# Block A's seven-product stage: one order in all groups, narrow columns first for three row pairs, weight and row sums in small parts

## The chip, the core and the metric

The kernel runs as one program on one core of a Trainium2 chip. The metric is the device time of one execution in microseconds. A core has five engines that run their own instruction queues side by side: TensorE (PE in the profile) multiplies matrices into eight PSUM banks, VectorE (DVE), ScalarE (ACT) and GpSimd (POOL) work elementwise, and SyncE (SP) issues the transfers between HBM and the on-chip memory. Each queue is worked off in order; an instruction that waits for another engine holds up all that stands behind it in its own queue.

## What is computed

Two attention blocks with 2048 rows, width 640 and 32 heads of 20, whose outputs stand side by side. Block A looks at eight earlier rows at distance 2, block B at all rows.

```
qkv = (x @ wqkv).reshape(B, S, 3, H, Dh)          # both blocks
A: logits[s, w] = q[s] . k[s - 2 w] * Dh**-0.5,  w = 0..7;  softmax over w;  o = sum attn * v
B: scores = q k^T * Dh**-0.5;  softmax over all keys;  o = p @ v
out = concat([o_A @ wo_A, o_B @ wo_B], axis=-1)
```

## The kernel before

Every matrix product is done in three passes, because a float32 value is kept as a rounded part ("hi") and a remainder ("lo"): hi*hi, hi*lo and lo*hi (`PASSES`). ACT casts the hi part and DVE subtracts it to get the lo part (`lo_of`); a pair of such instructions stands wherever an operand is prepared.

The program has, in this order: block A's projection `x @ wqkv` for the first 12 of 16 row tiles (the loop over `a_steps`), block B's query and key projection, its value projection, and then a long loop over block B's scores, maxima, exponentials and products, beside which POOL computes block A's window attention.

The change touches the first of these alone. There the columns of `wqkv` are held as two weight sets: `WP[0]` (W0, two halves of 512 columns) and `WP[1]` (W1, the narrow one, two halves of 448). The rows are held as six row pairs `XA[0..5]`, 256 rows each, two tiles of 128. The first 8 steps project the first two row pairs with W0 in the plain way. All that follows is done by `a_quad`, once for a row pair and a weight set: ten groups, each a 2x2 block product with seven products in place of eight. It needs sums of weight chunks (`ACols.sums`, four DVE instructions for each of two chunk pairs), their hi and lo parts (`ACols.second`: two casts on ACT, two remainders on DVE), the same of the rows (`ARows.sums`, `ARows.second`) and the parts of the unsummed rows (`ARows.base`: three casts, three remainders).

A group has 54 matmuls. By the names of the products, with the matmuls in each: A11 B11 (6), which ACT copies to `c[0]`; S4 with B22 (9); S2 T2 (6), after which DVE sets `c[1] = c[0] + b[1]`; A12 with B21 (9), into the bank that ACT has copied, and a store; S1 T1 (6), `c[1] += b[2]` and a store; S3 T3 (6), added in PSUM to the bank of S2 T2, `c[0] += b[1]`; then the last rows' chunk (three matmuls, added to the bank of S1 T1) and a store, and A22 with T4 (9) and a store. So S3 waits for DVE's first addition and the last chunk's three matmuls for its second. In the first group (`late`) A12 stands before S2.

A step (`n`) is what lies between two `yield`s of a group: four to a group, steps 8 to 11 are group 0, 12 to 15 group 1, and so on; step 47 is the last. One more place, "between", lies behind a group's first product, with `n` still that of the step before. Which preparation stands at which step is written out by hand, in the loop over `a_steps`: it sets where in the queues of ACT, DVE and SP the pieces come, in front of or behind the group's own copies and additions. A tile that is stored (`ro`) goes to DRAM one step later through SP's queue; three buffers hold them. The buffers "vb", two in number, are shared by the loaded rows (`stg`) and the weights' sums (`x_sums`). Two chunks of late weight columns are loaded in the stage (`late_w`, tile `wt`), cast some steps later, and stored with the rest of the weights (`keep`) for later use.

In the profile all recorded instructions carry line 61, that of the helper which records them, so they are told apart by tile: `sum` is c[0] or c[1], `wc` and `wl` weight parts, `wr` and `sums` weight sums, `xn` row parts, `stg` loaded rows.

Of the kernel before, what the change touches and what calls it, by code (L numbers as in the profile page):

```python
# [9 lines left out]
F32 = mybir.dt.float32  # L10
F32R = mybir.dt.float32r
AF = mybir.ActivationFunctionType
ALU = mybir.AluOpType
# [8 lines left out]
KC = 5  # L22
# [43 lines left out]
def attention_pair(ctx, tc, xa, wqk_a, wv_a, wo_a, xb, wqk_b, wv_b, wo_b, oa, ob):  # L66
# [3 lines left out]
    sb = ctx.enter_context(tc.tile_pool(name="sb", bufs=1))  # L70
# [3 lines left out]
    dve, act = InOrder(tc, nc.vector, 0.075, 960), InOrder(tc, nc.scalar, 0.111, 1400)  # L74
# [151 lines left out]
    class ARows:  # L226


        def __init__(self, p, raw=None):
            self.p, self.raw, self.rest = p, raw, None  # L230

        def load(self):
            self.raw = sb.tile([128, KC, 256], F32, tag="vb", bufs=2, name="stg")
            sp.dma_start(self.raw, xa[:, self.p * 256:self.p * 256 + 256].rearrange("(k p) c -> p k c", p=128))

        def parts(self, u, k, src):
# [24 lines left out]
            self.parts(self.u, 4, self.raw[:, 1:KC - 1:2, 128:])  # L261
            self.parts(self.u, 6, self.raw[:, KC - 1].rearrange("p (t c) -> p t c", t=2))

        def sums(self):
            ev, od = (self.raw[:, o:KC - 1:2] for o in range(2))
            a11, a12, a21, a22 = ev[:, :, :128], od[:, :, :128], ev[:, :, 128:], od[:, :, 128:]
            dve.tensor_tensor(a22, a21, a22, ALU.add)
            dve.tensor_tensor(a21, a11, a21, ALU.subtract)
            dve.tensor_tensor(a11, a22, a11, ALU.subtract)
            dve.tensor_tensor(a12, a12, a11, ALU.subtract)  # L270

        def second(self):
            hi, lo = (self.u[:, i, 8:].rearrange("p (k t) c -> p k t c", t=2) for i in range(2))
# [13 lines left out]
    class ACols:  # L287
# [65 lines left out]
            self.one(self.b11[kp], self.raw[2 * kp][:, 0])  # L353
            self.one(self.odd[kp], self.raw[2 * kp + 1])

        def sums(self, kp, x):

            ev, od = self.raw[2 * kp:2 * kp + 2]
            x = x[:, :, :self.n]
            dve.tensor_tensor(x[:, 0], ev[:, 1], ev[:, 0], ALU.subtract)  # L360
            dve.tensor_tensor(x[:, 1], od[:, 1], ev[:, 1], ALU.subtract)
            dve.tensor_tensor(od[:, 1], od[:, 1], x[:, 0], ALU.subtract)
            dve.tensor_tensor(od[:, 0], od[:, 0], od[:, 1], ALU.subtract)

        def second(self, kp, x):

# [40 lines left out]
    def product(p, xs, ws, start, stop):  # L407

        for n, (x, w) in enumerate(zip(xs, ws)):
            for i, (wi, xi) in enumerate(PASSES):  # L410
                pe.matmul(p, x(xi), w(wi), start=start and n == i == 0, stop=stop and n == len(ws) - 1 and i == 2,
                          skip_group_check=not start)

    def a_store(g, t, op, *srcs):

        r = sb.tile([128, WA], F32, tag="ao", bufs=3, name="ro")
        c, end = AC[g], AC[g + 1]
        op(r[:, :end - c], *(u[:, :end - c] for u in srcs))
        hf, r0 = divmod(t * 128, HS)
        while c < end:  # L420
            m, c1 = divmod(c, D)
            n = min(D - c1, end - c)
            dst, pad = ((qa_d, 0), (ka_d, PAD), (va_d, PAD))[m]
            after(1, sp.dma_start, dst[hf, pad + r0:pad + r0 + 128, c1:c1 + n], r[:, c - AC[g]:c - AC[g] + n])
            c += n

    def add(r, a, b):
        dve.tensor_tensor(r, a, b, ALU.add)
# [7 lines left out]
    def a_quad(X, W, late=False):  # L436

        n, t, g = W.n, 2 * X.p, 2 * W.P
        A11, A12 = ([X.rows(0, 2 * kp + o) for kp in range(2)] for o in range(2))
        A22 = [X.rows(1, 2 * kp + 1) for kp in range(2)]  # L440
        l1, l2 = ([X.rows(j, KC - 1)] for j in range(2))
        B11 = [W.cols(2 * kp, 0) for kp in range(2)]
        B21, B22 = ([W.cols(2 * kp + 1, j) for kp in range(2)] for j in range(2))
        b = [next_bank()[:, :n] for _ in range(5)]
        c = [sb.tile([128, 512], F32, tag=tag, bufs=2, name="sum")[:, :n] for tag in ("raw", "rb")]
        product(b[0], A11, B11, True, True)
        act.copy(c[0], b[0])
        yield True
        product(b[3], X.s(4) + l1, B22 + W.c[1], True, True)

        def c11():
            product(b[0], A12 + l1, B21 + W.c[0], False, True)
            a_store(g, t, act.copy, b[0])
        if late:
            c11()
            yield
        product(b[1], X.s(2), W.T(2), True, True)
        add(c[1], c[0], b[1])
        if not late:
            c11()  # L460
            yield
        product(b[2], X.s(1), W.T(1), True, True)
        add(c[1], c[1], b[2])
        a_store(g + 1, t, add, c[1], b[3])
        yield
        product(b[1], X.s(3), W.T(3), False, True)
        add(c[0], c[0], b[1])
        product(b[2], l2, W.c[1], False, True)
        a_store(g + 1, t + 1, add, c[0], b[2])
        yield  # L470
        product(b[4], A22 + l2, W.T(4) + W.c[0], True, True)
        a_store(g, t + 1, add, c[0], b[4])
        yield

    def store_rows(p, dst):
# [12 lines left out]
    XA = [ARows(p, r[0][:, 2:, p * 256:p * 256 + 256]) for p in range(2)]  # L488
    WP = [ACols(0, r[0][:, :2]), ACols(1, r[1][:, :2, :448])]
# [215 lines left out]
    def a_steps():  # L705

        W = WP[0]
        first = [next_bank() for _ in range(4)]
        for k in range(KC):
            W.half(k, 0)  # L710
            for x in XA:
                x.chunk(k)
            for c in PASSES:
                for t in range(4):
                    pe.matmul(first[t], XA[t // 2].rows(t % 2, k)(c[1]), W.cols(k, 0)(c[0]),
                              start=(k == 0 and c == PASSES[0]), stop=(k == KC - 1 and c == PASSES[-1]))
        for k in range(KC):
            W.half(k, 1)
        for x in XA:
            x.sums()  # L720
        for x in XA:
            x.second()
        for t in range(4):
            a_store(0, t, act.copy, first[t])
            yield
        for t in range(4):
            p = next_bank()
            product(p, [XA[t // 2].rows(t % 2, k) for k in range(KC)], [W.cols(k, 1) for k in range(KC)], True, True)
            a_store(1, t, act.copy, p)
            yield  # L730
        for p in range(2):
            yield from a_quad(XA[p], WP[1], not p)
        for p in range(2, UP // 2):
            for W in WP:
                yield from a_quad(XA[p], W)

    keeps = [(0, 0, 1), (0, 2, 1)]
# [3 lines left out]
    n = -1  # L741
    for between in a_steps():
        if between:
            if n == 7:
                WP[0].second(0, x_sums)
            elif n == 11:
                XA[2].base()
            continue
        tick()
        n += 1  # L750
        if n == 0:
            for j in range(2):
                WP[1].half(KC - 1, j)
        elif n == 1:
            WP[1].base(0)
            x_sums = sb.tile([128, 2, 512], F32, tag="vb", bufs=2, name="sums")
        elif n == 2:
            WP[1].sums(0, x_sums)
            WP[1].base(1)
        elif n == 3:  # L760
            WP[1].second(0, x_sums)
            WP[1].sums(1, x_sums)
        elif n == 6:
            WP[1].second(1, x_sums)
        elif n in (7, 8):
            WP[0].sums(n - 7, x_sums)
        elif n == 12:
            WP[0].second(1, x_sums)
        if n in (5, 13, 14, 21):
            XA.append(ARows(len(XA)))  # L770
            XA[-1].load()
        if n in (16, 24, 32):
            XA[n // 8 + 1].base()
        elif n in (12, 17, 25, 33):
            XA[n // 8 + 1].sums()
        elif n in (13, 18, 26, 34):
            XA[n // 8 + 1].second()
        if n in (33, 35):
            for c in range(n - 33, n - 31):
# [9 lines left out]
        if n in (16, 24):  # L789
            k = n // 4 - 4  # L790
            late_w = [sb.tile([128, WP[1].n], t, tag="aq", bufs=2, name="wt") for t in (F32, F32R)]
            sp.dma_start(late_w[0][:, :128], wv_a[0, :, k, 192:])
            sp.dma_start(late_w[0][:, 128:], wv_a[1, :, k])
        elif n in (20, 28):
            act.copy(late_w[1], late_w[0])
            lo_of(late_w[0].bitcast(F32R), late_w[0], late_w[1])
            late_w = [late_w[1], late_w[0].bitcast(F32R)]
        elif n in (21, 29):
            k = n // 4 - 5
            WP[1].b12 = {k // 2: late_w}  # L800
            WP[1].keep(k, 1)
        if n in (36, 37):
            pairs_x = [] if n == 36 else pairs_x
            pairs_x.append(x_raw(0, 2 * len(pairs_x), 2 * len(pairs_x) + 2, "vb", 2))
        elif n == 38:
            raw_m = [sb.tile([128, KC, 128], F32, tag="aq", bufs=2, name="stg") for _ in range(2)]
            for r, m in zip(raw_m, MS):
                sp.dma_start(r, wqk_b[m])
        elif n == 40:
            XB.append([big(0, [128, 2, KC - 1, 512], "xn"), None])  # L810
# [647 lines left out]
```

## Time and profile before

| | us |
|---|---|
| median of 3 runs | 1768.23 |
| lowest and highest | 1765.77, 1768.40 |
| the profiled execution | 1767.34 |
| its span, first to last instruction | 1765.6 |
| PE busy | 1739.2 |
| DVE, ACT, POOL busy | 1415.8, 1335.5, 1228.0 |

The seven-product groups run from about 33 to 168 us of the span; block B's projection begins at 168.21. The 40 slices of the page (44 us each) give the busy share in tenths; the stage lies in the first four.

```profile
PE   9899999999999999999999999999999999999999
PEld 7688888874445444444444444444444444444569
DVE  7545433689999999999999999999999999999400
ACT  6212322218998999999999999989999999989881
POOL 0000594495989888888898898988888898745442
PEclk9899999999999999999999999999999999999999
DMA  7468868784435563644474446536552635222223
```

A busy PE is not yet a PE at its full rate: a matmul's length is modelled, and the row PEclk says what clock was granted. A wait is given with the engine and the tile that ended it.

### The profile page before, as it was taken

Reading aid. Unit: us, or ns where it says so; the run is one execution under the profiler, and the core shown is the slowest. Engines: PE = TensorE matmul, PEld = TensorE weight load, DVE = VectorE, ACT = ScalarE, POOL = GpSimd, SP = SyncE. Lnnn points to the kernel's source line nnn. Section 1 sums busy time; section 2 is a strip of 40 time slices with the busy share of each in tenths; the row PEclk is TensorE's granted clock in tenths of the full one; section 3 lists DMA queues with packets and bytes.
Section 4 is the critical chain, followed back from the end, with each engine's and each line's share of the span. In section 5 each row is a group of like instructions: output and inputs, shape, how many; then the busy total and the mean of one; then the engine's idle time right before and its main releaser. Section 6 shows DMA issues by size and latency. Waiting matters only on the chain.

```text
span 1765.6 us, 32050 instructions
## 1 busy us (share of the span) xinstructions
PE 1739.2 (99%) x11271; PEld 991.9 (56%) x11271; DVE 1415.8 (80%) x1944; ACT 1335.5 (76%) x2601; POOL 1228.0 (70%) x1086
## 2 busy tenths in 40 slices
PE   9899999999999999999999999999999999999999
PEld 7688888874445444444444444444444444444569
DVE  7545433689999999999999999999999999999400
ACT  6212322218998999999999999989999999989881
POOL 0000594495989888888898898988888898745442
PEclk9899999999999999999999999999999999999999
DMA  7468868784435563644474446536552635222223
GB/s 228 144 201 268 311 245 269 228 258 114 150 115 158 136 183 114 156 144 133 137 187 139 133 148 155 166 100 173 140 165 90 147 106 144 60 73 62 61 71 111
DMA packets 220920, 270.19 MB, mean 153 GB/s; under 512 B 92748, under 2 KB 141400, under 8 KB 220760
## 3 DMA queue, kind: packets, MB, share of 16 engines
q1 hardware_dynamic: 220184, 267.50, 51.4%
q8 instruction: 88, 1.44, 0.3%
q14 instruction: 72, 0.59, 0.1%
q10 hardware_dynamic: 576, 0.66, 0.1%
HBM read 193.33 MB, written 74.74 MB: 152 GB/s over the span
## 4 chain that ended last, share of the span: by engine, by line
PE 91%; DVE 4%; DMA 1%; ACT 1%; issue 1%; SPq 1%; POOL 0%; DVEq 0%; ACTq 0%; POOLq 0%
PE ps_st L61 91%; DVE mx L61 2%; DMA bk<-kb_d 1%; SPq L61 1%; ACT e L61 1%; DVE wl L61 1%; DVE wr L61 0%; DMA wr<-wqk_a 0%; ACT wc L61 0%; DVE sums L61 0%; DVE xn L61 0%; DVE wc L61 0%; DMA rb<-s_d 0%; DVE sum L61 0%; POOL braw L61 0%
## 5 line engine op out<-in xcount | busy, mean ns | idle before, releaser
L61 DVE TENSOR_REDUCE mx<-ps_st 128x1 f32<-128x512 f32 (+1 forms) x1500 | 1217.5, 877 | 75.9 <-PE ps_st L61 65.6
L61 ACT ACTIVATE e<-ps_st 128x512 f32<-128x512 f32 x2048 | 1067.3, 609 | 34.0 <-PE ps_st L61 15.2
L61 PE MATMUL ps_st<-bq,bk 62*128 62x512 f32 x2048 | 610.7, 439 | 0.2
L61 PE MATMUL ps_st<-bk,bq 60*128 60x512 f32 x2048 | 556.9, 435 | 3.1 <-DMA bq<-qb_d 1.3
L61 PEld LDWEIGHTS ps_st<-bq,bk 62*128 62x128 f32 x2048 | 288.2, 184 | 478.4 <-ACT e L61 336.9
L61 PE MATMUL ps_st<-e,vb 128*32 128x512 f32 x4096 | 542.9, 604 | 2.1
L61 POOL TENSOR_TENSOR braw<-braw,more 128x512 f32<-128x512 f32 x224 | 287.7, 1284 | 145.6 <-ACT more L61 129.9
L61 POOL TENSOR_TENSOR akv<-akv 128x640 f32<-128x640 f32 (+3 forms) x304 | 282.1, 928 | 23.8
L61 PEld LDWEIGHTS ps_st<-bk,bq 60*128 60x128 f32 x2048 | 265.5, 184 | 35.8 <-DVE mx L61 12.0
L61 POOL TENSOR_TENSOR akv<-akv,aq 128x1280 f32<-128x1280 f32 x64 | 188.1, 2939 | 22.8 <-DMA akv<-ka_d 22.7
L61 PEld LDWEIGHTS ps_st<-e,vb 128*32 128x32 f32 x4096 | 82.0, 108 | 156.1 <-issue 71.0
L61 POOL TENSOR_TENSOR akv<-akv,al 128x1280 f32<-128x1280 f32 x64 | 152.1, 2376 | 0.2
L61 PE MATMUL ps_st<-wc,xn 128*128 128x512 f32 (+1 forms) x544 | 138.8, 388 | 13.4 <-DVE sum L61 12.1
L61 ACT COPY ro<-ps_st 128x320 f32<-128x320 f32 (+2 forms) x102 | 45.8, 451 | 137.0 <-PE ps_st L61 120.0
L61 ACT COPY more<-ps_st 128x512 f32<-128x512 f32 x224 | 132.5, 591 | 1.7 <-PE ps_st L61 1.4
L61 PE MATMUL ps_st<-ww,xn 128*128 128x320 f32 x768 | 125.8, 314 | 0.5 <-ACT e L61 0.5
L61 PEld LDWEIGHTS ps_st<-ww,xn 128*128 128x128 f32 x768 | 113.5, 188 | 20.8 <-ACT e L61 8.8
L61 PEld LDWEIGHTS ps_st<-wc,xn 128*128 128x128 f32 x544 | 104.8, 194 | 31.8 <-DVE sum L61 15.1
L61 POOL MEMSET ve<- 128x347 f32 x4 | 1.4, 391 | 168.4 <-DVE ro L61 156.7
L61 PE MATMUL ps_st<-xn,w 128*128 128x512 f32 x480 | 115.4, 389 | 0.0
L61 PEld LDWEIGHTS ps_st<-xn,w 128*128 128x128 f32 x480 | 90.0, 188 | 18.8 <-issue 0.2
L61 ACT CAST pr<-ps_st 128x512 fp32r<-128x512 f32 x40 | 23.5, 587 | 97.3 <-PE ps_st L61 93.1
(91 smaller groups left out, 1119.7 us busy)
## 6 DMA issues: line engine op xcount, KB each, us to landing
akv<-ka_d SPq DMA_DIRECT2D x128, 320.0 KB
akv<-va_d SPq DMA_DIRECT2D x128, 320.0 KB
wx<-wa_d SPq DMA_DIRECT2D x24, 480.0 KB
kb_d<-pr SPq DMA_DIRECT2D x20, 512.0 KB
qb_d<-pr SPq DMA_DIRECT2D x20, 512.0 KB
bk<-kb_d SPq DMA_DIRECT2D x16, 640.0 KB
bq<-qb_d SPq DMA_DIRECT2D x64, 160.0 KB
rb<-s_d SPq DMA_DIRECT2D x128, 64.0 KB
```

The lines of the kernel that those rows point to most:

```text
L61: return self.tc.keep_in_program_order(op(*a, **k))
```

## The change

Three things change, all in the seven-product stage. In every group the last two pieces change places: A22 with T4 stands before the last chunk's three matmuls. The third row pair, like the first two, takes W1 before W0, so that W0's sums are needed one group later. And the preparation moves to other steps: W1's last part behind group 0's first product; W0's four parts, which stood in groups 0 and 1, to steps 9 to 17, with one of the sums split in two; the rows' `base`, `sums` and `second` to behind the first product and the two steps after it, in the group before they are used; a row pair's buffer is taken apart from its load; the late columns' casts come one step earlier; some loads of block B's rows move by one to three steps.

```diff
-            for W in WP:
+            for W in (WP if p > 2 else WP[::-1]):
                 yield from a_quad(XA[p], W)
...
         add(c[0], c[0], b[1])
+        product(b[4], A22 + l2, W.T(4) + W.c[0], True, True)
+        a_store(g, t + 1, add, c[0], b[4])
+        yield
         product(b[2], l2, W.c[1], False, True)
         a_store(g + 1, t + 1, add, c[0], b[2])
-        yield
-        product(b[4], A22 + l2, W.T(4) + W.c[0], True, True)
-        a_store(g, t + 1, add, c[0], b[4])
         yield
...
         if between:
             if n == 7:
-                WP[0].second(0, x_sums)
+                WP[1].second(1, x_sums)
             elif n == 11:
                 XA[2].base()
+                XA[2].sums()
+            elif n == 15:
+                WP[0].sums(1, x_sums, 0)
+            elif n in (19, 27, 35):
+                XA[(n + 1) // 8 + 1].base()
             continue
...
         elif n == 1:
             WP[1].base(0)
+            XA.append(ARows(2))
+            XA[2].buffer()
             x_sums = sb.tile([128, 2, 512], F32, tag="vb", bufs=2, name="sums")
...
-        elif n == 6:
-            WP[1].second(1, x_sums)
-        elif n in (7, 8):
-            WP[0].sums(n - 7, x_sums)
+        elif n == 9:
+            WP[0].sums(0, x_sums)
         elif n == 12:
-            WP[0].second(1, x_sums)
-        if n in (5, 13, 14, 21):
+            XA[2].second()
+        elif n == 16:
+            WP[0].sums(1, x_sums, 1)
+        elif n in (14, 17):
+            WP[0].second(n // 17, x_sums)
+        if n in (13, 18, 23):
             XA.append(ARows(len(XA)))
+            XA[-1].buffer()
+        if n in (5, 13, 18, 23):
             XA[-1].load()
-        if n in (16, 24, 32):
-            XA[n // 8 + 1].base()
-        elif n in (12, 17, 25, 33):
+        if n in (20, 28, 36):
             XA[n // 8 + 1].sums()
-        elif n in (13, 18, 26, 34):
+        elif n in (21, 29, 37):
             XA[n // 8 + 1].second()
...
-        elif n in (20, 28):
+        elif n in (19, 27):
             act.copy(late_w[1], late_w[0])
...
-        if n in (36, 37):
-            pairs_x = [] if n == 36 else pairs_x
+        if n in (34, 38):
+            pairs_x = [] if n == 34 else pairs_x
...
-        elif n == 38:
+        elif n == 39:
             raw_m = [sb.tile([128, KC, 128], F32, tag="aq", bufs=2, name="stg") for _ in range(2)]
```

In `ACols.sums` and `ARows.sums` a parameter `part` picks the first two or the last two of the four instructions.

How the queues move is seen best in three places. On ACT, around the first product of group 0 (`sum` is its copy, the casts of 896 are W1's second part, those of 1024 W0's):

```order
 L61 CAST wc<-wr 128x896
 L61 CAST wc<-sums 128x896
-L61 COPY ro<-ps_st 128x512 x3
+L61 COPY ro<-ps_st 128x512 x4
+L61 COPY sum<-ps_st 128x448
 L61 CAST wc<-wr 128x896
 L61 CAST wc<-sums 128x896
-L61 COPY ro<-ps_st 128x512
-L61 COPY sum<-ps_st 128x448
-L61 CAST wc<-wr 128x1024
-L61 CAST wc<-sums 128x1024
```

The copy of the first product now stands ahead of the second pair of W1's casts, and W0's casts have left this place.

On DVE, in group 0 (`wl` of 896 are W1's remainders, `sums` and `wr` of 512 the sums of W0, `sum` and `ro` of 448 the group's own additions):

```order
 L61 TENSOR_TENSOR wl<-sums,wc 128x896
+L61 TENSOR_TENSOR sum<-sum,ps_st 128x448 x2
+L61 TENSOR_TENSOR ro<-sum,ps_st 128x448
 L61 TENSOR_TENSOR sums<-wr 128x512 x2
 L61 TENSOR_TENSOR wr<-wr,sums 128x512
 L61 TENSOR_TENSOR wr<-wr 128x512
-L61 TENSOR_TENSOR wl<-wr,wc 128x1024
-L61 TENSOR_TENSOR wl<-sums,wc 128x1024
-L61 TENSOR_TENSOR sums<-wr 128x512 x2
-L61 TENSOR_TENSOR wr<-wr,sums 128x512
-L61 TENSOR_TENSOR wr<-wr 128x512
-L61 TENSOR_TENSOR sum<-sum,ps_st 128x448 x2
```

The group's first two additions, which stood behind two parts of sums and one of remainders of W0, now stand ahead of all of them.

On PE, at the end of a W1 group (`wl` is the third pass of a T product; before, the first three of the five are the last chunk's):

```order
 L61 MATMUL ps_st<-wl,xn 128x448
-L61 MATMUL ps_st<-wc,xn 128x448 x5
-L61 MATMUL ps_st<-wl,xn 128x448
-L61 MATMUL ps_st<-wc,xn 128x448 x2
-L61 MATMUL ps_st<-wl,xn 128x448
-L61 MATMUL ps_st<-wc,xn 128x448 x3
+L61 MATMUL ps_st<-wc,xn 128x448 x2
+L61 MATMUL ps_st<-wl,xn 128x448
+L61 MATMUL ps_st<-wc,xn 128x448 x2
+L61 MATMUL ps_st<-wl,xn 128x448
+L61 MATMUL ps_st<-wc,xn 128x448 x6
```

The last chunk's three matmuls have gone from the front of the piece to its end, behind the nine of A22 with T4. Behind the stage, the rows of all engines are the same as before.

More of the change, by code (lines that the diff above doesn't have):

```diff
@@ L230, in __init__, with buffer @@
             self.p, self.raw, self.rest = p, raw, None
+        def buffer(self):
+            self.raw = sb.tile([128, KC, 256], F32, tag="vb", bufs=2, name="stg")
         def load(self):
-            self.raw = sb.tile([128, KC, 256], F32, tag="vb", bufs=2, name="stg")
             sp.dma_start(self.raw, xa[:, self.p * 256:self.p * 256 + 256].rearrange("(k p) c -> p k c", p=128))
@@ L262, in base, with sums @@
             self.parts(self.u, 6, self.raw[:, KC - 1].rearrange("p (t c) -> p t c", t=2))
-        def sums(self):
+        def sums(self, part=None):
             ev, od = (self.raw[:, o:KC - 1:2] for o in range(2))
             a11, a12, a21, a22 = ev[:, :, :128], od[:, :, :128], ev[:, :, 128:], od[:, :, 128:]
[L267 to L270, printed above, removed]
+            if part != 1:
+                dve.tensor_tensor(a22, a21, a22, ALU.add)
+                dve.tensor_tensor(a21, a11, a21, ALU.subtract)
+            if part != 0:
+                dve.tensor_tensor(a11, a22, a11, ALU.subtract)
+                dve.tensor_tensor(a12, a12, a11, ALU.subtract)
         def second(self):
@@ L354, in base, with sums @@
             self.one(self.odd[kp], self.raw[2 * kp + 1])
-        def sums(self, kp, x):
+        def sums(self, kp, x, part=None):
             ev, od = self.raw[2 * kp:2 * kp + 2]
             x = x[:, :, :self.n]
[L360 to L363, printed above, removed]
+            if part != 1:
+                dve.tensor_tensor(x[:, 0], ev[:, 1], ev[:, 0], ALU.subtract)
+                dve.tensor_tensor(x[:, 1], od[:, 1], ev[:, 1], ALU.subtract)
+            if part != 0:
+                dve.tensor_tensor(od[:, 1], od[:, 1], x[:, 0], ALU.subtract)
+                dve.tensor_tensor(od[:, 0], od[:, 0], od[:, 1], ALU.subtract)
         def second(self, kp, x):
```

## The prediction

> **What bounds the kernel now.** I read the page first, for the engine that never rests, then who keeps that engine waiting.
>
> ```profile
> PE 1739.2 (99%) x11271; PEld 991.9 (56%) x11271; DVE 1415.8 (80%) x1944; ACT 1335.5 (76%) x2601; POOL 1228.0 (70%) x1086
> ...
> PE ps_st L61 <- DVE sum L61: 12.1, 6, 5.8
> ```
>
> The first row is of the page, the second of the view of waits (in all, times, longest). PE is the bound. Among its waits, DVE's `sum` (the additions of the seven-product stage) has 12.1 us in six waits, the longest 5.8. The timeline of PE (start, length, instruction, idle time before) places them, and one more for a copy of ACT; of the four short ones the first and the last are shown:
>
> ```profile
> 32.20 4.56 PE L61 MATMUL ps_st<-wc,xn 128*128 128x512 f32 x21
> 38.06 2.50 PE L61 MATMUL ps_st<-wc,xn 128*128 128x448 f32 x11 [1.30 <-ACT sum L61]
> ...
> 48.38 1.12 PE L61 MATMUL ps_st<-wc,xn 128*128 128x448 f32 x2 [5.79 <-DVE sum L61]
> ...
> 52.21 0.37 PE L61 MATMUL ps_st<-wl,xn 128*128 128x448 f32 x1
> ...
> 53.02 4.21 PE L61 MATMUL ps_st<-wc,xn 128*128 128x448 f32 x20
> 57.08 0.36 PE L61 MATMUL ps_st<-wl,xn 128*128 128x448 f32 x1
> ...
> 66.31 2.23 PE L61 MATMUL ps_st<-wc,xn 128*128 128x448 f32 x5 [4.01 <-DVE sum L61]
> ...
> 75.42 0.39 PE L61 MATMUL ps_st<-wl,xn 128*128 128x512 f32 x1
> ...
> 81.76 1.43 PE L61 MATMUL ps_st<-wc,xn 128*128 128x512 f32 x5 [0.51 <-DVE sum L61]
> ...
> 117.32 1.28 PE L61 MATMUL ps_st<-wc,xn 128*128 128x448 f32 x5
> ...
> 123.72 0.39 PE L61 MATMUL ps_st<-wl,xn 128*128 128x512 f32 x1
> ...
> 154.37 1.45 PE L61 MATMUL ps_st<-wc,xn 128*128 128x512 f32 x5 [0.80 <-DVE sum L61]
> ```
>
> Idle: 1.30 + 12.1 = **13.4 us**, of which 5.79 and 4.01 are the long waits and 12.1 - 9.8 = 2.3 the four short ones. The two long waits cost more than their length, because matmuls behind them run slowly. The windows view (length, PE busy, PEld, DVE, ACT, POOL, granted clock, DMA share, GB/s) shows the clock:
>
> ```profile
> 48.40:52.20 3.80, 3.80 (x11) 3.46 (x12) 2.05 (x4) 0.00 (x0) 0.00 (x0) 0.57 0.16 60
> ...
> 66.30:72.00 5.70, 5.68 (x15) 4.97 (x16) 3.54 (x5) 0.51 (x1) 0.00 (x0) 0.50 0.67 198
> ...
> 38.00:168.20 130.20, 117.99 (x525) 101.44 (x526) 68.27 (x110) 27.24 (x46) 0.72 (x2) 0.95 0.60 193
> ...
> 168.20:304.00 135.80, 135.80 (x600) 112.50 (x600) 50.55 (x65) 37.72 (x61) 86.07 (x76) 1.00 0.80 279
> ```
>
> Full-clock spacing at 448 columns is (57.08 - 53.02) / 20 = 0.203 us. From 48.38 to 52.21 stand 11 matmuls, 3.83 us where 2.23 were due: 1.60 lost. From 66.31 to 75.42 stand 29 matmuls, 9.11 us; the same 29 of a later group take 123.72 - 117.32 = 6.40: 2.71 lost. Slow clock: **4.31 us**. The stage holds 13.4 + 4.31 = 17.7 us that a dense PE wouldn't need.
>
> [...]
>
> **The change, part by part.** The number of matmuls, additions and casts is the same; what changes is which of them stand in front of what.
>
> *The first copy (1.30).*
>
> ```profile
> 35.31 0.94 ACT L61 CAST wc<-wr 128x896 fp32r<-128x896 f32 x1 [3.01 <-DVE wr L61]
> 36.15 0.93 ACT L61 CAST wc<-sums 128x896 fp32r<-128x896 f32 x1
> ...
> 37.47 0.54 ACT L61 COPY sum<-ps_st 128x448 f32<-128x448 f32 x1
> ```
>
> ACT casts `W1.second(1)`, waits inside for DVE, and then copies the first product, for which PE waits. The change puts the copy ahead. PE's 21 matmuls end at 32.20 + 4.56 = 36.76 and the last nine (9 x 0.203 = 1.83) come behind the first product, which is thus ready at about 35.0; one `ro` copy and this one take about 1.1 us, done by 36.2. The wait goes. The casts follow until about 38.1, DVE's two remainders (1.09 each, as below) until about 39.3. The first is wanted 14 matmuls after 36.76, at 39.6, the second 1.2 us later; both are there over 1 us earlier.
>
> *The long wait (5.79 + 1.60).*
>
> ```profile
> 37.48 1.09 DVE L61 TENSOR_TENSOR wl<-sums,wc 128x896 fp32r<-128x896 f32 x1
> 38.60 1.29 DVE L61 TENSOR_TENSOR sums<-wr 128x512 f32<-128x512 f32 x2
> ...
> 47.10 0.69 DVE L61 TENSOR_TENSOR wr<-wr 128x512 f32<-128x512 f32 x1
> 47.71 1.34 DVE L61 TENSOR_TENSOR sum<-sum,ps_st 128x448 f32<-128x448 f32 x2
> ```
>
> From 38.60 to 47.71 DVE works on W0's weights, and only then adds what PE waits for. All of it moves behind. The S2 product then ends at 36.76 + 15 x 0.203 = 39.8, its addition (0.62) at 40.5, and S3, which adds into that bank, is due after six more matmuls, at 41.0. The wait goes, with 0.5 us to spare: the thinnest margin here.
>
> *The second long wait (4.01 + 2.71).*
>
> ```profile
> 56.13 1.36 DVE L61 TENSOR_TENSOR xn<-stg,xn 128x512 fp32r<-128x512 f32 x3 [1.62 <-ACT xn L61]
> ...
> 61.47 1.22 DVE L61 TENSOR_TENSOR wl<-wr,wc 128x1024 fp32r<-128x1024 f32 x1 [2.76 <-ACT wc L61]
> 62.79 1.23 DVE L61 TENSOR_TENSOR wl<-sums,wc 128x1024 fp32r<-128x1024 f32 x1
> 63.94 1.80 DVE L61 TENSOR_TENSOR stg<-stg 128x256 f32<-128x256 f32 x4
> ...
> 66.84 1.22 DVE L61 TENSOR_TENSOR xn<-stg,xn 128x1024 fp32r<-128x1024 f32 x1
> ```
>
> W0's remainders wait for ACT, then four row sums run, then the addition of group 1. After the change DVE has, from step 9 to step 17, two sums of W0 (2 x 2.6, 1.29 as at 38.60 and two of 0.69), two remainders (2 x 2.45), row pair 2 (1.36 + 1.80 + 1.22): 14.5 us. Its own work for a group is six of 0.62, 3.7 us. From step 9 of group 0 to step 17 of group 2 are about two groups of 54 x 0.203 = 11.0 us plus 2.5, less than 25 us, and they have to hold 14.5 + 2.2 x 3.7 = 22.7 us. It fits, at over 90%, so single additions will stand behind a piece of up to 2.45 us. Two things cover that: ACT, which makes the casts ahead of the remainders, is busy 27.24 us of 130.2, and in each group the nine matmuls of A22 (1.83) now stand between S3 and the last three, whose bank needs the addition. I take 0.4 us as left; the ends are 0 (all margins hold) and 6.7 (the same wait comes back whole).
>
> *The four short waits (2.3).*
>
> ```profile
> 79.74 1.36 DVE L61 TENSOR_TENSOR xn<-stg,xn 128x512 fp32r<-128x512 f32 x3 [2.46 <-ACT xn L61]
> 81.02 0.68 DVE L61 TENSOR_TENSOR sum<-sum,ps_st 128x512 f32<-128x512 f32 x1
> ```
>
> In each W0 group the three remainders of the next rows delay the two additions before the last product. The exchange puts nine matmuls, at least 9 x 0.203 = 1.8 us, in front of the matmuls that wait, at most 0.80 until now. They go. The next to be late would be S3, for the addition behind S2; from group 1 on it has fifteen matmuls of cover (nine of A12, six of S1), 3.0 us or more.
>
> *Transfers and later stages.* Behind the stage every engine has the same rows in the same order; POOL has no difference at all. PE is busy 135.80 of the next 135.80 us, so its end moves as the stage's end does, and nothing is given back unless data come late. DMA's work from 38.00 to 168.20 is 0.60 x 130.2 = 78 us; in 17.3 us less it is a share of 0.69. It is the burst that could bite:
>
> ```profile
> 169.51 0.62 ACT L61 CAST xl<-stg 128x512 fp32r<-128x512 f32 x1 [4.14 <-DMA stg<-xb]
> ...
> 171.00 0.84 PE L61 MATMUL ps_st<-xl,w 128*128 128x512 f32 x3
> ```
>
> The load for `xl` stands at the same step as before, so its lead stays; cast and remainder are done barely ahead of 171.00. Being later costs PE one for one; I take 0; the ends are 0 and 2, half of the 4.14 that ACT waits there.
>
> **Sum.** 13.4 + 4.31 - 0.4 = 17.3 us off the profiled execution's own 1767.34 (span 1765.6): 1750.0 us. The median of the runs is 1768.23, 0.9 above that execution, so the forecast against the median is 1750 to 1751; I say 1750.
>
> **The rivals.** *DVE or a load becomes the new wait (15 in 100).* Where the margins of 0.5 us break, part comes back. The other place is ACT's cast of the late weight columns, one step earlier than before:
>
> ```profile
> 79.64 0.88 SPq L61 DMA_DIRECT2D wt<-wv_a x2
> ...
> 91.36 0.57 ACT L61 CAST wt<-wt 128x448 fp32r<-128x448 f32 x1
> ...
> 147.49 0.49 SPq L61 DMA_DIRECT2D stg<-xb x1
> ...
> 153.48 1.05 ACT L61 CAST xn<-stg 128x1024 fp32r<-128x1024 f32 x1 [1.02 <-DMA stg<-xb]
> ```
>
> It came 11.7 us behind its issue; a step is (154.37 - 81.76) / 24 = 3.0 us, so 8.7 remain, and a 512 KB load took 5.5 (147.98 to 153.48). Behind the cast stands the copy of the next group's first product, with 15 matmuls (3.0) of cover. Both casts 3 us beyond that, or the wait of 4.01 with its 2.71 again, is 6 to 7 us: 1756.5. Against it speaks that each cover is longer than the rows it has to hide.
>
> *Slower (4 in 100): the order of stores.*
>
> ```profile
> 145.97 0.62 DVE L61 TENSOR_TENSOR ro<-sum,ps_st 128x448 f32<-128x448 f32 x1 [3.01 <-DMA va_d<-ro]
> ```
>
> DVE can stand at a store's buffer until an earlier store has left through SP's queue, and with it the additions behind. PE meets it at the next S3, 36 matmuls on, so it decides from 36 x 0.203 = 7.3 us; at 9.5 us in each of the eight later groups the gain is gone (8 x 2.2). If the shorter stage makes SP lag to 11.3 us, each loses 4.0 and, as behind the wait of 4.01, 2.7 of slow clock: 8 x 6.7 = 54 us, 1804. Against it: the longest such wait is 3.01, once, and it held up no matmul.
>
> *No change (4 in 100).* DVE's work is only moved, so the same 17 us of waiting could appear at the new places: about 1767. For it speaks DVE's over 90% in groups 0 to 2; against, the same DVE has 68.27 of 130.2 us in the whole stage.
>
> **Chances.** Forecast 77, partial 15, same 4, slower 4. A measurement of this kernel tells about 0.2% (3.5 us) from no change, so the partial case counts as faster: faster 92, same 4, slower 4. The range: down to 1747 (nothing left, and the fastest run lies 2.5 under the median), up to 1757 (the partial case); beyond it lie the last two cases and a tail.
>
> **What would show it.** Right: no wait of PE for `sum` above 1 us between 36 and 151; the granted clock 1.00 in that stretch; the first matmul of the next stage at about 151 instead of 168.21; later stages alike. Wrong: a wait for DVE between 40 and 65, a wait of ACT at `wt` that PE shares, or `xl` late at the stage's end.

## The result and the profile after

| | before | after |
|---|---|---|
| median, us | 1768.32 | 1749.12 |
| lowest and highest of 4 runs | 1765.77, 1768.56 | 1747.40, 1750.89 |
| the profiled execution | 1767.34 | 1747.40 |
| its span | 1765.6 | 1745.6 |

The time after is 0.9895 of the time before (0.9878 to 0.9912): 19.2 us less by the medians, where 17.3 were forecast against the profiled execution and 18.2 against the median. The forecast time, 1750, lies 0.9 above the median measured. Executions whose mean granted clock was 0.85 (one of the kernel before, 1868.31 us, and the profiled one of the exchange alone, 1861.01) are left out of every ratio, and the second is read for no length of the stage.

The page of the changed kernel shows the same work, and a whole clock in the first slices (the line of busy times, then the granted clock in the 40 slices):

```profile
PE 1733.5 (99%) x11271; PEld 988.5 (57%) x11271; DVE 1414.7 (81%) x1944; ACT 1335.8 (77%) x2601; POOL 1229.4 (70%) x1086
...
PEclk9999999999999999999999999999999999999999
```

PE's busy time fell by 5.7 us although the number of matmuls is the same: by the prediction's count 4.31 of that is the slow clock, which made matmuls long. The digit 8 in the second slice of PEclk is gone with it. The view of waits (in all, times, longest) has no row for DVE's `sum` any more; its longest is now one wait that was there before:

```profile
PE ps_st L61 <- POOL ident L61: 1.4, 1, 1.4
PE ps_st L61 <- DVE mx L61: 0.9, 2, 0.6
PE ps_st L61 <- DMA bq<-qb_d: 0.5, 1, 0.5
```

The timeline of PE (start, length, instruction) at the two ends of the stage: the last products of the plain steps with the first of group 0, and the first matmuls of block B's projection.

```profile
32.10 6.79 PE L61 MATMUL ps_st<-wc,xn 128*128 128x512 f32 x32
...
148.16 2.97 PE L61 MATMUL ps_st<-xn,w 128*128 128x512 f32 x12
150.96 1.11 PE L61 MATMUL ps_st<-xl,w 128*128 128x512 f32 x3
151.91 2.91 PE L61 MATMUL ps_st<-xn,w 128*128 128x512 f32 x12
154.66 0.84 PE L61 MATMUL ps_st<-xl,w 128*128 128x512 f32 x3
155.34 0.84 PE L61 MATMUL ps_st<-xn,w 128*128 128x512 f32 x3
```

Between the same two points lay 168.21 - 32.20 = 136.01 us before and lie 148.16 - 32.10 = **116.06** now: 19.95 less. From the second point to the span's end it is 1765.6 - 168.21 = 1597.4 before and 1745.6 - 148.16 = 1597.4 now. So between these two executions the whole gain was made in the stage, and in sum nothing was given back behind it. This length of the stage is used below as the measure of each experiment, since it has no part in what happens later.

The windows view (length, then busy time of PE, PEld, DVE, ACT and POOL, granted clock, DMA share, GB/s) shows a dense PE at full clock:

```profile
42.83:66.59 23.76, 23.76 (x119) 22.00 (x118) 20.82 (x34) 8.00 (x12) 0.00 (x0) 1.00 0.59 191
...
34.00:150.50 116.50, 116.50 (x549) 102.69 (x548) 71.86 (x115) 30.56 (x51) 0.72 (x2) 1.00 0.71 228
```

### The profile page after: what moved, and what is told of

The parts are those of the page before. It is cut to its first block, busy times and chain, and to the rows that moved or that the text cites. A ratio compares the mean times of both kernels' runs of the same rounds, so it can differ in the third digit from the quotient of the medians.

```text
span 1745.6 us, 32037 instructions
## 1 busy us (share of the span) xinstructions
PE 1733.5 (99%) x11271; PEld 988.5 (57%) x11271; DVE 1414.7 (81%) x1944; ACT 1335.8 (77%) x2601; POOL 1229.4 (70%) x1086
## 4 chain that ended last, share of the span: by engine, by line
PE 91%; POOL 3%; DVE 2%; ACT 2%; DMA 1%; issue 1%; SPq 0%; POOLq 0%; DVEq 0%; ACTq 0%
PE ps_st L61 91%; POOL akv L61 2%; DVE mx L61 2%; ACT e L61 1%; POOL braw L61 1%; DMA bk<-kb_d 1%; DMA vb_d<-ve 0%; ACT more L61 0%; POOL xn L61 0%; POOL al L61 0%; POOL ao L61 0%; POOL aot L61 0%; DVE mtr L61 0%; SPq L61 0%; POOL am L61 0%
## 5 line engine op out<-in xcount | busy, mean ns | idle before, releaser
L61 PE MATMUL ps_st<-wc,xn 128*128 128x512 f32 (+1 forms) x544 | 133.6, 378 | 0.0
```

Of the source, the lines that this page charges most:

```text
L61: return self.tc.keep_in_program_order(op(*a, **k))
```

## The experiments

The theory was that of the prediction: each wait went because a piece of ACT's or DVE's work now stands behind the addition or copy that PE needs, or because matmuls now stand in front of those that wait. Two things it left open: which of the three moves does what, and what a wait costs beside its length. All kernels are the changed one with one or two parts undone or something added, except the exchange alone, which is the kernel before with one part done. The stage's length is taken between the two points used above, and is compared with 116.06 of the changed kernel and 136.01 of the one before. The exchange alone has no row in the table. Four kernels were executed once ("single"), so for them the stage's length is the measure, not the time.

| run | median or single time | stage, us | over the changed kernel's |
|---|---|---|---|
| old order of the last pieces | 1753.14 | 150.07 - 31.36 = 118.71 | 2.65 |
| the same, and rows at their old steps | 1753.65 | 152.52 - 31.40 = 121.12 | 5.06 |
| W0's parts at their old steps | 1758.87 | 158.62 - 31.54 = 127.08 | 11.02 |
| rows at their old steps | 1747.78 | 148.26 - 31.57 = 116.69 | 0.63 |
| third pair with W0 first | 1753.59 | 150.86 - 32.26 = 118.60 | 2.54 |
| W1's last part ahead of the copy | 1752.24, single | 151.88 - 31.48 = 120.40 | 4.34 |
| sums in one piece | 1749.58 | 147.57 - 31.51 = 116.06 | 0.00 |
| late load two steps later | 1756.10, single | 156.23 - 31.58 = 124.65 | 8.59 |
| additions repeated, long | 1770.22, single | 169.34 - 31.75 = 137.59 | 21.53 |
| additions repeated, short | 1760.23, single | 156.04 - 32.14 = 123.90 | 7.84 |

**The old order of the last two pieces.**

```diff
         add(c[0], c[0], b[1])
-        product(b[4], A22 + l2, W.T(4) + W.c[0], True, True)
-        a_store(g, t + 1, add, c[0], b[4])
-        yield
         product(b[2], l2, W.c[1], False, True)
         a_store(g + 1, t + 1, add, c[0], b[2])
+        yield
+        product(b[4], A22 + l2, W.T(4) + W.c[0], True, True)
+        a_store(g, t + 1, add, c[0], b[4])
         yield
```

> The changed kernel with A22 and T4 again behind the last chunk's three matmuls in every group; all else as changed. If the exchange is what removed the four short waits, they come back (0.7 to 1.0 us each by the matmuls' starts, and about 1.1 in group 1): 4 to 4.5 us more than the changed kernel, about 1753.5. If moving the rows' pieces behind the first product removed them already, only the last W0 group (no row pieces left, block B's halves in front) and group 1 wait, about 1 us each: about 1751. My guess is the second.

Measured: a ratio of 0.9917 (0.9899 to 0.9935) to the kernel before. The timeline of PE has two waits for `sum`, in group 1 and in the last W0 group, as the second account had it (its total, 1751, is missed; more on that at the end of this section):

```profile
53.31 1.29 PE L61 MATMUL ps_st<-wc,xn 128*128 128x448 f32 x5 [0.98 <-DVE sum L61]
...
136.25 1.43 PE L61 MATMUL ps_st<-wc,xn 128*128 128x512 f32 x5 [0.80 <-DVE sum L61]
```

The short waits of the groups between did not come back. So the exchange is not what removed them there, or not it alone: the other candidate is the move of the rows' pieces.

**The old order with the rows' pieces at their old steps**, the same edit and this one:

```diff
-            elif n in (19, 27, 35):
-                XA[(n + 1) // 8 + 1].base()
...
-        if n in (20, 28, 36):
+        if n in (16, 24, 32):
+            XA[n // 8 + 1].base()
+        elif n in (17, 25, 33):
             XA[n // 8 + 1].sums()
-        elif n in (21, 29, 37):
+        elif n in (18, 26, 34):
             XA[n // 8 + 1].second()
```

> The changed kernel with the old order in a group and the rows' base, sums and second at the old steps (16, 24, 32 and on); weights as changed. Either account of the short waits has them back here: three waits of about 0.7 to 1.0 us in W0 groups and about 1 us each in groups 1 and 2, 4 to 5 us more than the changed kernel, about 1753.5. If less than 1.5 us come back, both accounts fall and the short waits came from the weights' place.

Measured: 0.9921 (0.9905 to 0.9937). The view of waits has five now, and the timeline shows the three that are new (one of them here):

```profile
PE ps_st L61 <- DVE sum L61: 3.5, 5, 1.0
...
90.38 1.43 PE L61 MATMUL ps_st<-wc,xn 128*128 128x512 f32 x5 [0.52 <-DVE sum L61]
```

It stands in the W0 group of the fourth row pair, at the place of this wait of the kernel before:

```profile
105.90 1.43 PE L61 MATMUL ps_st<-wc,xn 128*128 128x512 f32 x5 [0.52 <-DVE sum L61]
```

With both undone it is back; with the exchange alone undone it was not.

**The rows' pieces at their old steps, the exchange kept** (only the second edit).

> The changed kernel with the rows' base, sums and second at the old steps (16, 24, 32 and on), the exchange and everything else as changed. If the exchange alone covers the short waits (nine matmuls against waits under 1.2 us), the stage stays dense but for at most 0.5 us behind group 2: 1749 to 1750.5, PE's waits for sums under 0.6 us in all. If the rows' place was needed too, at least two waits of 0.7 us or more stand in the W0 groups: 1751 or more.

Measured: 0.9892 (0.9875 to 0.9908), a stage 0.63 longer, and one wait, for ACT's copy:

```profile
71.03 2.79 PE L61 MATMUL ps_st<-wc,xn 128*128 128x512 f32 x11 [0.34 <-ACT sum L61]
```

No wait for DVE's `sum`. So each of the two edits alone covers the waits of the middle groups, and the exchange covers the other two besides. The rows' move is worth 0.6 us where the exchange is made, which the total doesn't tell from nothing. Both runs undo it for the last three row pairs only; the third pair's pieces (steps 11 and 12) stayed where the change put them.

**The exchange alone in the kernel before.**

```diff
         add(c[0], c[0], b[1])
+        product(b[4], A22 + l2, W.T(4) + W.c[0], True, True)
+        a_store(g, t + 1, add, c[0], b[4])
+        yield
         product(b[2], l2, W.c[1], False, True)
         a_store(g + 1, t + 1, add, c[0], b[2])
-        yield
-        product(b[4], A22 + l2, W.T(4) + W.c[0], True, True)
-        a_store(g, t + 1, add, c[0], b[4])
         yield
```

> The kernel before with the exchange of the two last pieces alone. If each wait has its own cause, the four short waits go (by the matmuls' starts 3.4 us with the slow first matmul behind each), the wait of 4.01 shrinks by the nine matmuls of cover to about 2.3 with less slow clock behind it, and the wait of 5.79 and the copy's 1.30 stay: 6 to 8 us less than before, 1760.5 to 1762.5. If the exchange were the main part of the change: 1755 or less.

Measured: 1761.44 against 1768.19 of the kernel before on the same chip, 0.9966 (0.9953 to 0.9979); this reading rests on the times alone. Made alone, the exchange is worth 6 to 7 of the 19 us, as forecast; undone in the changed kernel it cost 2.65 of the stage. What it is worth depends on which other moves are made, so the prices of the parts don't add up.

**W0's parts at their old steps**, with W1's last part at step 6 as before; the narrow columns still first.

```diff
-                WP[1].second(1, x_sums)
+                WP[0].second(0, x_sums)
...
-            elif n == 15:
-                WP[0].sums(1, x_sums, 0)
...
-        elif n == 9:
-            WP[0].sums(0, x_sums)
+        elif n == 6:
+            WP[1].second(1, x_sums)
+        elif n in (7, 8):
+            WP[0].sums(n - 7, x_sums)
...
         elif n == 12:
+            WP[0].second(1, x_sums)
+        elif n == 13:
             XA[2].second()
-        elif n == 16:
-            WP[0].sums(1, x_sums, 1)
-        elif n in (14, 17):
-            WP[0].second(n // 17, x_sums)
```

> The changed kernel with W1's last part and W0's sums and parts at their old steps (6 to 8 and 12), so in front of group 0's additions; exchange, narrow columns first and rows as changed. My account: the copy's wait (1.5 by starts), the long wait (6.0) and its slow clock (about 2) come back, and at most 0.6 in group 1: 9 to 10.5 us more than the changed kernel, 1758 to 1760. If the order in a group had freed DVE enough, under 3 us come back: below 1752.

Measured: 0.9951 (0.9936 to 0.9966), the stage 11.02 longer. The timeline of PE has the copy's wait and the long wait again (a third, 0.48 at 65.12, is not shown):

```profile
38.55 4.04 PE L61 MATMUL ps_st<-wc,xn 128*128 128x448 f32 x11 [2.45 <-ACT sum L61]
...
48.88 1.12 PE L61 MATMUL ps_st<-wc,xn 128*128 128x448 f32 x2 [4.26 <-DVE sum L61]
```

DVE's timeline shows the cause of the second: from 39.10 on it works on W0's weights, and the addition follows at 48.22, as it did at 47.71 in the kernel before.

```profile
39.10 1.29 DVE L61 TENSOR_TENSOR sums<-wr 128x512 f32<-128x512 f32 x2
...
48.22 1.34 DVE L61 TENSOR_TENSOR sum<-sum,ps_st 128x448 f32<-128x448 f32 x2
```

**W1's last part alone ahead of the copy**, to price the first term by itself.

```diff
-            if n == 7:
-                WP[1].second(1, x_sums)
-            elif n == 11:
+            if n == 11:
...
+        elif n == 6:
+            WP[1].second(1, x_sums)
```

> The changed kernel with W1's second part at step 6 again, in front of group 0's first product, and nothing else undone. My account: the copy of that product waits behind two casts, PE stands 1.3 us idle as before (1.5 by the matmuls' starts), no slow clock behind it, the stage ends 1.4 to 1.7 us later than the changed kernel's 148.16. If the copy's wait was only a share of the long one: no wait above 0.3 us.

Measured: the stage 4.34 longer, three times what the wait of 1.30 in the kernel before had cost. The timelines of PE and ACT and the windows view:

```profile
38.54 4.06 PE L61 MATMUL ps_st<-wc,xn 128*128 128x448 f32 x11 [2.50 <-ACT sum L61]
42.43 0.37 PE L61 MATMUL ps_st<-wl,xn 128*128 128x448 f32 x1
...
37.95 0.53 ACT L61 COPY sum<-ps_st 128x448 f32<-128x448 f32 x1
...
38.50:42.50 4.00, 3.96 (x12) 3.55 (x13) 0.55 (x1) 0.44 (x1) 0.00 (x0) 0.57 0.80 275
```

The wait is a race between PE, which reached group 0 at 31.48 here and at 32.20 before (0.72 earlier), and ACT, which copied at 37.95 here and at 37.47 before (0.48 later): 1.30 + 0.72 + 0.48 = 2.50. And behind 2.50 the clock fell: 11 matmuls took 42.43 - 38.54 = 3.89 in place of 11 x 0.203 = 2.23, which is 1.66 more. The mechanism was as stated, its size was not fixed by the order alone.

**The third row pair with W0 first.**

```diff
-            for W in (WP if p > 2 else WP[::-1]):
+            for W in WP:
...
-            elif n == 15:
-                WP[0].sums(1, x_sums, 0)
...
-        elif n == 16:
-            WP[0].sums(1, x_sums, 1)
-        elif n in (14, 17):
-            WP[0].second(n // 17, x_sums)
+        elif n in (13, 14):
+            WP[0].sums(1, x_sums, n - 13)
+        elif n in (10, 15):
+            WP[0].second(n // 15, x_sums)
```

> The changed kernel with the third row pair's W0 group before its W1 group again, so W0's four pieces one group earlier (steps 9, 10, 13, 14 and 15). If DVE's share was the reason for the narrow columns first (14.5 us of pieces and the additions in less than two groups is over 90 percent already), PE waits again in groups 1 and 2, about 1 us each by the lanes: 2 to 3 us more than the changed kernel, 1751 to 1752, PE waiting for DVE between 48 and 65 us. If the place of the pieces alone mattered, no wait above 0.3 us: 1749.

Measured: 0.9921 (0.9906 to 0.9936), the stage 2.54 longer, with two waits in the timeline of PE:

```profile
53.31 0.68 PE L61 MATMUL ps_st<-wc,xn 128*128 128x448 f32 x2 [1.28 <-DVE sum L61]
...
62.41 0.50 PE L61 MATMUL ps_st<-wl,xn 128*128 128x512 f32 x1 [0.53 <-DVE wl L61]
```

The second is a matmul that waits for a weight remainder itself. One group earlier, more of W0's 10.1 us of DVE work (2 x 2.6 + 2 x 2.45, the prediction's rows) stands ahead of the addition behind the first wait, which DVE starts at 52.64 instead of 50.24, and a remainder of W0 is late itself. Another placing of the four pieces in this order of groups was not tried.

**W0's second sums in one piece**, at step 16 instead of half behind group 1's first product.

```diff
-            elif n == 15:
-                WP[0].sums(1, x_sums, 0)
...
-            WP[0].sums(1, x_sums, 1)
+            WP[0].sums(1, x_sums)
```

> The changed kernel with W0's second sums in one piece at step 16, not in two halves at 15 and 16. My account: four instructions of 0.69 us in one place (2.7 us) still fit under the fifteen matmuls of cover, so the stage ends within 0.2 us of 148.16 and the time is that of the changed kernel. If the small parts matter: a wait of PE of 0.5 us or more between 56 and 65 us.

Measured: 0.9894 (0.9878 to 0.9911), the stage as long as in the changed kernel to the hundredth, and no wait for `sum`. The split of the sums is worth nothing here; the cover is wide enough for the whole piece.

**The late weights' loads two steps later**, for the rival in which a load becomes the new wait.

```diff
-        if n in (16, 24):
+        if n in (18, 26):
```

> The changed kernel with the loads of the late weight columns two steps later (18 and 26), so 6 us less lead ahead of the cast, the rival of the prediction. In the changed kernel ACT stands 2.64 and 4.83 us for them and PE not at all. If the cover is what I worked out (15 matmuls, 3.0 to 3.4 us, behind the copy that waits), 6 us less leaves PE waiting 1.5 to 4 us at each, 4 to 8 us in all with slow clock, and DVE and ACT late behind. If the loads have 6 us to spare, nothing changes: 1749.

Measured: the stage 8.59 longer. The timelines of ACT and PE, and the windows view behind the first wait:

```profile
73.38 0.56 ACT L61 CAST wt<-wt 128x448 fp32r<-128x448 f32 x1 [9.80 <-DMA wt<-wv_a]
...
74.48 5.06 PE L61 MATMUL ps_st<-wc,xn 128*128 128x512 f32 x11 [3.77 <-ACT sum L61]
...
103.02 2.50 PE L61 MATMUL ps_st<-wc,xn 128*128 128x448 f32 x11 [1.59 <-ACT sum L61]
...
74.40:80.00 5.60, 5.51 (x13) 4.36 (x14) 3.77 (x9) 2.39 (x6) 0.00 (x0) 0.50 0.05 14
```

ACT stands at the late load, the copy of the next first product stands behind it, and PE waits for that copy, as the rival had it; behind 3.77 us the clock is at half for over 5 us, behind 1.59 it is not (11 matmuls in 2.50). In the changed kernel ACT waits at the same cast, but not long enough for PE to notice:

```profile
66.74 0.57 ACT L61 CAST wt<-wt 128x448 fp32r<-128x448 f32 x1 [2.64 <-DMA wt<-wv_a]
```

So the margin there is real and less than 5 us wide: SP issued the first of these loads at 68.73 instead of 63.78, 4.95 later.

**Additions repeated**, to price a wait by its length. In the W0 groups of row pairs 3, 4 and 5 the addition behind S2 is done 9, 11 and 14 times, and in a second kernel 6, 7 and 8 times.

```diff
-        add(c[1], c[0], b[1])
+        for _ in range({(3, 0): 9, (4, 0): 11, (5, 0): 14}.get((X.p, W.P), 1)):
+            add(c[1], c[0], b[1])
```

> The changed kernel with the addition behind the S2 product done 9, 11 and 14 times (the same sum again, harmless) in the W0 groups of row pairs 3, 4 and 5, so that PE waits there. By DVE's 0.73 us for one that waits for the last, PE stands 3.5, 4.9 and 7.2 us. The times of matmuls behind tell what a wait of known length costs in slow clock. By my reading of the profile before: about 1.6 to 2.9 us of slow clock behind each. [...] In all 20 to 24 us more than the changed kernel.

> As the last, with 6, 7 and 8 additions: PE stands about 1.3, 2.0 and 2.7 us. [...] The wait of 2.45 us in the run with W0's pieces early was followed by matmuls at 0.37 us: if that is the rule, the longest here, perhaps the second, is followed by 2 to 3 us lost to slow clock: 8 to 11 us slower.

Measured: waits of 3.22, 4.66 and 6.82 us in the long one and of 1.06, 1.78 and 2.50 in the short one. The windows of the short one, behind its second wait and then in two pieces behind its third:

```profile
113.30:117.00 3.70, 3.70 (x16) 3.06 (x17) 2.07 (x4) 0.00 (x0) 0.00 (x0) 1.00 0.22 74
139.30:140.30 1.00, 1.00 (x5) 0.83 (x6) 1.00 (x2) 0.00 (x0) 0.00 (x0) 0.99 0.93 348
140.30:143.60 3.30, 3.30 (x9) 2.62 (x8) 3.07 (x5) 0.00 (x0) 0.00 (x0) 0.50 0.50 181
```

Behind 1.78 the clock stays whole. Behind 2.50 PE works a whole microsecond at full clock and then falls to half, for 3.3 us. In the long kernel the fall comes 1.5 us behind the first wait, at 91.20, and has come before PE resumes behind the other two (windows in the last section).

Three waits of 14.70 us in all cost 21.53, three of 5.34 cost 7.84: half again what the list of waits says, in both. The short kernel has one lapse of the clock in that, the long one three. So a wait cost its listed length, a part that was alike at each (in the short kernel 0.15 or 0.16 at the wait, counted from start to start, and 0.12 or 0.13 in the five matmuls behind each of the first two), and a lapse of the clock behind some of them (the last section says which). The 7.84 lies just under the 8 to 11 forecast for the short kernel, with a lapse behind its longest wait alone.

What these runs leave open: in the kernels with old order, wide third pair and short repetition, the part behind the stage was about 5 us longer in the profiled execution (1752.6 - 150.07 = 1602.5 in the first) than in the changed kernel. The view of waits of the first names two tiles of the later stages, which had 0.9 and 0.5 in the changed kernel:

```profile
PE ps_st L61 <- DVE mx L61: 2.5, 4, 1.2
PE ps_st L61 <- DMA bq<-qb_d: 1.9, 1, 1.9
```

Its mean granted clock is 0.998, against 1.000 in the changed kernel. Why these waits come in some executions was not tried. They are why a total of one execution says less here than the stage's length.

Some moves were never undone by themselves: a row pair's buffer apart from its load, the late columns' casts one step earlier, the loads of block B's rows, and the third row pair's pieces. The runs can't say whether they were needed.

## Why the prediction was right, step by step

**The first copy.** Forecast: done by 36.2, the casts' remainders by 39.3, over 1 us ahead of need. ACT's timeline has the copy and DVE's the last remainder:

```profile
34.87 0.53 ACT L61 COPY sum<-ps_st 128x448 f32<-128x448 f32 x1
...
38.06 1.09 DVE L61 TENSOR_TENSOR wl<-sums,wc 128x896 fp32r<-128x896 f32 x1
39.74 0.62 DVE L61 TENSOR_TENSOR sum<-sum,ps_st 128x448 f32<-128x448 f32 x1 [0.58 <-PE ps_st L61]
```

The copy is done at 35.40, the remainder at 39.15. Right; the run with that part alone undone shows that the place matters, at 4.34 rather than 1.30.

**The long wait.** The first addition was forecast to be done at 40.5, half a microsecond before S3. It is done at 39.74 + 0.62 = 40.36, and S3 starts (PE's timeline) at 40.75:

```profile
40.75 0.57 PE L61 MATMUL ps_st<-wc,xn 128*128 128x448 f32 x2
```

So the thinnest margin is 0.39 us, and it holds. That this term, with the copy's, was the larger part is shown by the run with W0's parts at their old steps.

**The second long wait.** From W0's first sum at 42.83 to the end of its last remainder at 66.59 DVE is busy 20.82 of 23.76 us, 88%, where 22.7 in under 25, over 90%, were forecast. That was right, and the **0.4 us** left for single additions behind a piece did not appear. The runs show the cover is wider than argued: neither the split of the sums nor the later rows' move was needed for it, while the third pair's order was.

**The four short waits.** They went. The reason given, nine matmuls of cover, is enough alone (rows at their old steps) but not the only one: the rows' move covers the middle groups without it. The prediction gave all of it to the exchange.

**Transfers and later stages.** DMA's share was forecast at 0.69 and is 0.71. The `xl` load was taken at 0, with ends 0 and 2: its first three matmuls took 151.91 - 150.96 = 0.95, the next three 155.34 - 154.66 = 0.68, so 0.27 are lost. The later stages are alike, 1597.4 us in both.

**The sum** was too small: the next stage begins at 148.16, not at about 151, and the term that was mis-sized is the idle time of 13.4. It was read from the list of waits, which counts from the modelled end of the matmul ahead. Counted from start to start it is more. Rows of the kernel before, each the last ahead of a wait (the seventh of the first row starts at 35.18 + 6 x 0.203 = 36.40), and one behind a wait:

```profile
35.18 1.58 PE L61 MATMUL ps_st<-wc,xn 128*128 128x448 f32 x7
...
42.22 0.37 PE L61 MATMUL ps_st<-wl,xn 128*128 128x448 f32 x1
...
80.86 0.39 PE L61 MATMUL ps_st<-wl,xn 128*128 128x512 f32 x1
...
83.02 0.39 PE L61 MATMUL ps_st<-wl,xn 128*128 128x512 f32 x1
```

Less one spacing of 0.203 (0.227 at 512 columns: three in 155.34 - 154.66 = 0.68), the waits at 38.06, 48.38 and 81.76 lost 1.46, 5.96 and 0.67 us, each 0.16 or 0.17 more than the 1.30, 5.79 and 0.51 that were listed. Over seven waits that is 1.1. The five matmuls behind the last of these take 83.02 - 81.76 = 1.26 in place of 5 x 0.227 = 1.14, another 0.12; behind the two long waits this is in the 4.31 already, so five times 0.12 gives 0.6. With these and the 0.4 that was not left, 17.3 becomes 17.3 + 0.4 + 1.1 + 0.6 = 19.4 of the 19.95 measured. Most of the rest is two waits too short for the list: at 93.17 and 117.32 of the kernel before PE starts 0.26 behind the matmul ahead where 0.203 is due, and the five matmuls that follow take 1.12 in place of 1.02, together 0.3; about 0.2 stay unassigned. That the median lies only 0.9 from the forecast is in part luck: the profiled execution after, 1747.40, is 2.6 below the 1750.0 forecast for it, and the median of its kernel is 1.7 above it.

**The rivals.** A load as the new wait is a real place, shown by the run with the later loads, and not reached here. The room worked out for it was wrong: 8.7 us from issue to cast were forecast, but SP issued the load at 63.78 and the cast started at 66.74, 2.96 later, after ACT had waited 2.64 for it. PE was not held up, because the copy behind the cast still had to wait 0.56 us for PE's product. The order of stores didn't bite: PE has no wait for `sum` left behind which a store could stand. "No change" fell with the full clock and the missing row of waits.

## What to carry to other kernels

In a queue that is worked off in order, the preparation of later operands belongs behind the instruction that the bound engine is waiting for. It paid twice where that engine's clock had fallen with the wait: the 5.79 and 4.01 us of waiting in the kernel before came with 4.31 us of slow clock. Of a bundle of such moves some may do all the work: here the weight parts' places, the order of row and column groups and the exchange of two pieces carried it, while the move of the later rows and the split of the sums covered what was covered already. Price a wait from the start of one matmul to the start of the next, not from the list of idle times, and compare stages rather than whole executions.

## What the runs showed of the hardware

PE's granted clock fell to half behind some waits of this stage and not behind others. It fell behind 2.45 and 4.26 us (W0's parts at their old steps), 2.50 (W1's last part ahead of the copy, and the short repetition), 3.22, 4.66 and 6.82 (the long repetition), 3.77 (the late load), 4.01 and 5.79 (the kernel before), and not behind 1.30 (the kernel before), 1.59 (the late load) or 1.78 (the short repetition). None of the waits read here lies between 1.78 and 2.45.

When it fell differs too. With W1's last part ahead of the copy the clock is whole from 36.00 to 38.50, and PE resumes at 38.54 into a slow one:

```profile
36.00:38.50 2.50, 0.04 (x1) 0.00 (x0) 1.64 (x2) 2.48 (x4) 0.00 (x0) 1.00 0.62 150
38.50:42.40 3.90, 3.86 (x11) 3.46 (x12) 0.55 (x1) 0.34 (x1) 0.00 (x0) 0.56 0.82 282
```

In the two kernels of repeated additions the fall came 1.0 us (behind 2.50) and 1.5 us (behind 3.22) after PE had resumed, and behind 4.01, 4.66, 5.79 and 6.82 us it came while PE was still waiting. The stretches at half clock in the kernel before and in the long kernel of repeated additions (taken up to 0.01 us inside their ends):

```profile
44.87:51.69 6.82, 3.31 (x9) 3.00 (x10) 5.21 (x9) 0.00 (x0) 0.00 (x0) 0.50 0.16 57
65.35:72.17 6.82, 5.86 (x15) 5.12 (x16) 4.46 (x7) 1.04 (x1) 0.00 (x0) 0.50 0.59 175
...
91.21:94.61 3.40, 3.40 (x9) 2.63 (x8) 0.69 (x1) 0.03 (x1) 0.00 (x0) 0.50 0.54 177
...
118.51:125.32 6.81, 5.80 (x14) 4.54 (x15) 2.99 (x5) 0.00 (x0) 0.00 (x0) 0.50 0.29 80
...
149.23:156.04 6.81, 3.49 (x8) 2.81 (x9) 6.64 (x10) 0.00 (x0) 0.00 (x0) 0.50 0.03 9
```

They last 6.82, 6.82, 3.40, 6.81 and 6.81 us, and PE works in them, at half clock, for 3.31, 5.86, 3.40, 5.80 and 3.49. So what a lapse cost was not in proportion to the wait: behind 4.01 us PE worked slowly for 5.86, behind 6.82 us for 3.49. What sets the moment of the fall and the length of the slow stretch these runs don't show.

A wait at one place is not a constant of the order. With ACT's casts ahead of the first copy, PE waited 1.30 us in the kernel before and 2.50 in the changed kernel with that one part undone, because PE's arrival had moved by 0.72 us and ACT's copy by 0.48; and behind the longer wait the clock fell, which made 4.34 of it.
